# Top-k attention and a gated feed-forward: the comparison with the 32nd largest score moves from VectorE to GpSimd

## The chip, the core and the metric

The kernel runs on one core of a Trainium2 chip. A core has a matrix engine (TensorE, PE in the profile), a vector engine (VectorE, DVE), an engine for activation functions and copies (ScalarE, ACT), GpSimd (POOL) and a queue that issues transfers (SyncE, SP). Each engine works through its own instructions in program order, and they wait for one another through semaphores. The metric is the time of one execution on the device in microseconds (us), as the median of several runs; less is better. Beside the runs there is one profiled execution, from which all the lines of the profile come.

## What is computed

There are two parts. Attention over 8 batches and 8 heads, with 576 positions and a head size of 64, keeps for each query only the 32 largest scores; its output becomes the rows of a feed-forward layer of 4608 tokens, 512 wide, with 1536 hidden units.

```python
scores = scale * np.matmul(q, k.transpose(0, 1, 3, 2))          # scale = 1/8
kth = np.partition(scores, -32, axis=-1)[..., -32:-31]           # the 32nd largest
mask = scores >= kth
scores = np.where(mask, scores, -1e9)
attn = np.exp(scores - scores.max(-1, keepdims=True))
attn = attn / (attn.sum(-1, keepdims=True) + 1e-9)
x = np.matmul(attn, v)                                           # then (B,H,S,D) -> (B*S, H*D)
g = x @ w_gate
out = (g / (1 + np.exp(-g))) * (x @ w_val) @ w_out
```

All of it is float32.

## The kernel before

**Units.** Attention is cut into units of one batch, one tile of 128 queries and one pair of heads. 576 is four tiles of 128 and a rest of 64, so for each batch and pair there are four units of 128 queries with two heads each, and a fifth in which the 64 remaining queries of both heads share the 128 partitions, which then counts as one head. That makes 160 units, 128 with two heads and 32 with one. A head's scores are a row of 576 in each partition.

**A unit's way through the engines.** `scores` (L278) multiplies on TensorE and ScalarE copies the scores into the tile `sc`, which has two buffers. `select` (L316) works on VectorE alone: four rounds for each head, in which MAX8 (L329) finds the eight largest values and MATCH_REPLACE8 (L333) takes them out, so that the last value of the tile `m` is the 32nd largest. At the end of `select`, L339 writes a penalty into the tile `e`: the score is compared with the 32nd largest, and the result of the comparison, 1 or 0, is multiplied by FAR, -3e38. `penalize` (L343) works on GpSimd: it makes the bias for the exponential from the largest score (L349) and adds the scores to the penalty (L351), in one instruction for both heads, in place in `e`. `weigh` (L354) is the exponential on ScalarE with the sum of each row; `normalize` (L368) takes the reciprocal on VectorE (L372) and multiplies on ScalarE (L375). `turn` (L377) transposes the weights on TensorE (L387) and copies them back with ScalarE (L388), and `values` (L398) multiplies with v and writes the result to the feed-forward's input `xT`.

**The feed-forward.** `feed` (L457) works on blocks of 256 tokens, 18 in all. The first products (L471) go to gate and value; ScalarE evaluates them (L496 to L503) and GpSimd multiplies (L499, L504). The second product, with `w_out`, is done in full for the first block (L517). For all others it is done by a scheme with seven partial products instead of eight (L557), for which GpSimd forms differences and sums of the hidden values beforehand (L564, L572, L577, L605) and sums of the results afterwards (L543). `piece` hands out parts of this work, whose cost is counted in credits; `on_act` and `on_pool` are lists of ScalarE and GpSimd work that is put off until they are flushed.

**The weights.** Until about 190 us the 36 pieces of the weights are loaded and rounded to a shorter mantissa, in three steps on ScalarE (L114 to L117), VectorE (a shift, L121) and GpSimd (L122, L123). They are handed out between the rounds of `select`, five of them for every two units.

**The order.** The loop at L729 writes out by hand in which order each engine meets its instructions; the last lines of the kernel fix it. In step n, VectorE selects in unit n; GpSimd first does `penalize` for unit n-1, then the feed-forward work that is put off in `on_pool`; ScalarE copies for `turn(n-3)` and `values(n-4)`, then does the exponential of unit n-1, then the score copies of unit n+1, then what the feed-forward needs, and the normalization of unit n-2. TensorE does the transposes of unit n-3, the values of unit n-4, the scores of unit n+1, and then pieces of the feed-forward. The tile `e` has four buffers and `m` has two. No transfer is issued from GpSimd.

Of the kernel before, what the change touches and what calls it, by code (L numbers as in the profile page):

```python
# [9 lines left out]
ALU = mybir.AluOpType  # L10
FP32 = mybir.dt.float32
# [4 lines left out]
P = 128  # L16
TOP_K = 32
LOWEST = -3.4028234663852886e38
FAR = -3.0e38
# [6 lines left out]
def kernel(  # L26
# [37 lines left out]
    nc = tc.nc  # L64
    B, H, S, D = q.shape
# [16 lines left out]
    work = ctx.enter_context(tc.tile_pool(name="work", bufs=2))  # L82
# [189 lines left out]
    state = {}  # L272

    def n_heads(qt):

        return 1 if qt == J else 2
# [39 lines left out]
    def select(n):  # L316

        nh = n_heads(units[n][1])
        sc = state[n]["sc"]
        m = small.tile([P, 2, TOP_K], FP32, tag="m", name="m", bufs=2)  # L320
        heads = [slice(t * S, (t + 1) * S) for t in range(nh)]
        rest = work.tile([P, 2 * S], FP32, tag="rest", name="rest", bufs=1)
        e = work.tile([P, 2 * S], FP32, tag="e", name="e", bufs=4)
        state[n] |= dict(m=m, e=e, heads=heads)
        cur = sc
        rounds = TOP_K // 8
        for r in range(rounds):
            for t, hs in enumerate(heads):
                nc.vector.max(m[:, t, 8 * r : 8 * r + 8], cur[:, hs])  # L329
                yield  # L330
            if r < rounds - 1:
                for t, hs in enumerate(heads):
                    nc.vector.match_replace(  # L333
                        rest[:, hs], m[:, t, 8 * r : 8 * r + 8], cur[:, hs], LOWEST
                    )
                    yield
                cur = rest
        for t, hs in enumerate(heads):
            nc.vector.tensor_scalar(  # L339
                e[:, hs], sc[:, hs], m[:, t, TOP_K - 1 : TOP_K], FAR, ALU.is_lt, ALU.mult  # L340
            )

    def penalize(n):  # L343

        st = state[n]
        sc, m, e, heads = st.pop("sc"), st.pop("m"), st["e"], st["heads"]
        nh = len(heads)
        bias = small.tile([P, 2], FP32, tag="bias", name="bias")
        nc.gpsimd.tensor_scalar_mul(bias[:, 0:nh], m[:, 0:nh, 0], -scale)  # L349
        every = slice(0, nh * S)  # L350
        nc.gpsimd.tensor_tensor(e[:, every], e[:, every], sc[:, every], ALU.add)  # L351
        st["bias"] = bias
# [376 lines left out]
    for n in range(NU + VALUES):  # L729
        nh = n_heads(units[n][1]) if n < NU else 1  # L730
        topk = select(n) if n < NU else no
        over[n - 1] = normalize(n - 1) if 0 <= n - 1 < NU else no
        nxt = scores(n + 1) if n + 1 < NU else no
# [17 lines left out]
        if 0 <= n - 1 < NU:  # L751
            penalize(n - 1)
# [84 lines left out]
```

## Time and profile before

| | |
|---|---|
| median of 3 runs | 1821.28 us (1821.05 to 1821.64) |
| span of the profiled execution | 1817.8 us |
| mean granted TensorE clock | 0.967 of full speed |
| ScalarE busy | 1218.7 us, 67% of the span |
| VectorE: MAX8, MATCH_REPLACE8, the comparison | 817.7, 634.6 and 177.2 us busy |
| GpSimd: score addition L351, products L499 and L504 | 383.1 and 277.8 us busy |
| transfers | 59.65 MB, mean 33 GB/s |

The span runs from the first to the last instruction of the profiled execution; the runs' times also hold what lies before and after it. In the page, a group of instructions is given by its line in the kernel, the engine, the operation and the tiles it writes and reads; then come the number of instructions, the busy time, the mean duration in ns, and the engine's idle time just before them with what ended most of it. In a timeline the columns are start, time until the end (both in us), engine, line, operation, tiles, and in brackets the idle time before with its releaser. Consecutive instructions of a kind are merged there into one line with their number. The slices cut the span into forty equal parts; a digit is the busy share in tenths, and 9 means 90% or more.

### The profile page before, as it was taken

The page shows a single profiled execution, that of the slowest core. Times are in us where ns is not written, and L with a number is a line of the kernel's source. Part 1 is how long each engine was busy: PE and PEld are TensorE (multiplying, and loading weights), DVE is VectorE, ACT ScalarE, POOL GpSimd, SP SyncE. Part 2 cuts the span into 40 slices and gives each one's busy share as a digit, 9 for nine tenths or more (in the row PEclk, how much of TensorE's full clock was granted, in tenths as well). Part 3 has the DMA queues.
Part 4 walks back from the last instruction along what each step waited for, and adds up shares of the span by engine and source line. Part 5 has one row for each costly group of instructions (what it writes and reads, how often), then busy time and mean ns, then how long its engine had stood idle before and what let it go on. Part 6 is the DMA issues. An engine that isn't in the chain of part 4 may idle for free.

```text
span 1817.8 us, 30526 instructions
## 1 busy us (share of the span) xinstructions
PE 1708.7 (94%) x10756; PEld 1409.2 (78%) x10756; DVE 1610.7 (89%) x3372; ACT 1218.7 (67%) x2977; POOL 1036.4 (57%) x930
## 2 busy tenths in 40 slices
PE   4458999899999899999999999999999999999999
PEld 2346778687788788887888878887888878888887
DVE  7999999999999799997999989998999989998400
ACT  6778666676667676666767676767676766675532
POOL 5788756455565645554455636564556554646354
PEclk6669999899999999999999999999999999999999
DMA  7432030002100030000300021000300011000000
GB/s 191 125 108 90 14 85 7 12 1 50 45 1 13 2 82 12 13 1 22 73 12 2 13 56 39 1 12 3 74 19 13 1 36 33 1 13 12 1 12 12
DMA packets 109305, 59.65 MB, mean 33 GB/s; under 512 B 88544, under 2 KB 96992, under 8 KB 109152
## 3 DMA queue, kind: packets, MB, share of 16 engines
q1 hardware_dynamic: 108016, 57.37, 12.1%
q8 instruction: 85, 1.39, 0.3%
q14 instruction: 68, 0.56, 0.1%
q10 hardware_dynamic: 1136, 0.33, 0.1%
HBM read 48.23 MB, written 9.44 MB: 32 GB/s over the span
## 4 chain that ended last, share of the span: by engine, by line
PE 86%; DVE 8%; ACT 2%; POOL 2%; issue 2%; DMA 0%; SPq 0%; ACTq 0%; POOLq 0%
PE f L471 41%; PE x_ps L557 9%; PE av L416 8%; PE etps L387 7%; PE s L308 7%; PE y_ps L557 7%; DVE m L329 3%; DVE rest L333 3%; PE s L294 2%; PE av L407 1%; PE o_ps L517 1%; PE kqps L263 1%; DVE size L121 1%; DVE e L339 0%; POOL p L543 0%
## 5 line engine op out<-in xcount | busy, mean ns | idle before, releaser
L329 DVE MAX8 m<-rest 128x8 f32<-128x576 f32 x864 | 612.7, 744 | 2.2
L351 POOL TENSOR_TENSOR e<-e,sc 128x1152 f32<-128x1152 f32 (+1 forms) x160 | 383.1, 2394 | 83.7 <-DVE e L339 76.3
L333 DVE MATCH_REPLACE8 rest<-m,rest 128x576 f32<-128x576 f32 x576 | 423.1, 740 | 0.0
L471 PE MATMUL f<-xT,wg 128*128 128x256 f32 x1728 | 401.6, 382 | 0.0
L471 PE MATMUL f<-xT,wv 128*128 128x256 f32 x1728 | 399.1, 382 | 0.0
L471 PEld LDWEIGHTS f<-xT,wg 128*128 128x128 f32 x1728 | 323.1, 190 | 62.6 <-issue 21.3
L471 PEld LDWEIGHTS f<-xT,wv 128*128 128x128 f32 x1728 | 324.5, 190 | 58.7 <-issue 16.6
L499 POOL TENSOR_TENSOR h<-h,half_g 128x512 f32<-128x512 f32 x108 | 138.2, 1280 | 292.7 <-ACT h L498 292.2
L329 DVE MAX8 m<-sc 128x8 f32<-128x576 f32 x288 | 205.0, 747 | 104.0 <-ACT sc L299 57.8
L388 ACT COPY et<-etps 128x512 f32<-128x512 f32 (+1 forms) x448 | 184.1, 483 | 131.0 <-PE etps L387 130.2
L360 ACT ACTIVATE e<-e,bias 128x576 f32<-128x576 f32 x288 | 222.1, 777 | 57.5 <-POOL e L351 57.2
L387 PE MATMUL etps<-ident,e 128*128 128x128 f32 (+1 forms) x1312 | 184.5, 286 | 79.3 <-POOL size L122 18.2
L504 POOL TENSOR_TENSOR h<-h,val 128x512 f32<-128x512 f32 x108 | 139.6, 1293 | 186.3 <-ACT val L503 186.1
L387 PEld LDWEIGHTS etps<-ident,e 128*128 128x128 f32 (+1 forms) x1312 | 159.6, 147 | 106.0 <-POOL size L122 20.7
L375 ACT ACTIVATE e<-e,tot 128x576 f32<-128x576 f32 x288 | 212.0, 790 | 0.9 <-DVE tot L372 0.9
L333 DVE MATCH_REPLACE8 rest<-m,sc 128x576 f32<-128x576 f32 x288 | 211.5, 740 | 0.0
L308 PE MATMUL s<-kqT 64*128 64x288 f32 x1024 | 178.8, 449 | 14.1 <-ACT kqT L268 8.3
L339 DVE TENSOR_SCALAR e<-sc,m 128x576 f32<-128x576 f32 x288 | 177.2, 651 | 3.4
L416 PE MATMUL av<-et,v 128*64 128x128 f32 (+1 forms) x2560 | 170.3, 278 | 0.0
L313 ACT COPY sc<-s 128x288 f32<-128x288 f32 x512 | 164.0, 402 | 2.9 <-PE s L308 2.9
L496 ACT ACTIVATE h<-f 128x512 f32<-128x512 f32 x108 | 65.2, 604 | 133.3 <-PE f L471 133.3
L416 PEld LDWEIGHTS av<-et,v 128*64 128x64 f32 x2560 | 134.1, 143 | 22.8 <-issue 6.8
(73 smaller groups left out, 2029.1 us busy)
## 6 DMA issues: line engine op xcount, KB each, us to landing
v<-in_v_dram SPq DMA_DIRECT2D x32, 256.0 KB, 2.9
kq_in<-in_k_dram SPq DMA_DIRECT2D x63, 128.0 KB, 2.8
kq_in<-in_q_dram SPq DMA_DIRECT2D x63, 128.0 KB, 3.0
w<-in_moe_w_gate_dram SPq DMA_DIRECT2D x12, 512.0 KB, 3.7
w<-in_moe_w_val_dram SPq DMA_DIRECT2D x12, 512.0 KB, 3.8
w<-in_moe_w_out_dram SPq DMA_DIRECT2D x12, 512.0 KB, 3.5
out_dram<-o SPq DMA_DIRECT2D x38, 128.0 KB, 2.4
out_dram<-o SPq DMA_DIRECT2D x16, 256.0 KB, 2.4
```

Of the source, the lines that this page charges most:

```text
L308: nc.tensor.matmul(ps[:, 0:half], slab[d, q0 : q0 + P], slab[d, k0 : k0 + half])
L329: nc.vector.max(m[:, t, 8 * r : 8 * r + 8], cur[:, hs])
L333: nc.vector.match_replace(rest[:, hs], m[:, t, 8 * r : 8 * r + 8], cur[:, hs], LOWEST)
L339: nc.vector.tensor_scalar(e[:, hs], sc[:, hs], m[:, t, TOP_K - 1 : TOP_K], FAR, ALU.is_lt, ALU.mult)
L351: nc.gpsimd.tensor_tensor(e[:, every], e[:, every], sc[:, every], ALU.add)
L360: nc.scalar.activation(e[:, hs], e[:, hs], AF.Exp, bias=bias[:, t : t + 1], scale=scale, accum_out=tot[:, t : t + 1],)
L375: nc.scalar.mul(e[:, hs], e[:, hs], tot[:, t : t + 1])
L387: nc.tensor.transpose(ps[0:kl, c * P : (c + 1) * P], e[:, k0 : k0 + kl], ident[:])
L388: nc.scalar.copy(et[0:kl, c0 : c0 + cn, :], ps[0:kl, 0 : cn * P].rearrange("p (c j) -> p c j", c=cn),)
L416: nc.tensor.matmul(av[hh * R : (hh + 1) * R, 0:ql], v_last[:, hh, :] if c == J else vt[:, hh, c, :], moving, start=last and c == 0, stop=c ...
L471: nc.tensor.matmul(ps[:, i, :], w[:, kc, m * P : (m + 1) * P], x[:, kc, :], start=(kc == 0), stop=(kc == KC - 1),)
L557: nc.tensor.matmul(ps, lhsT, T[i][m], start=m == 0, stop=m == MQ - 1)
```

## The change

The comparison is no longer the last step of `select` on VectorE but is done on GpSimd in `penalize`, between the bias and the addition. The operation, its operands and its shape, one instruction for each head, stay the same. The tile `e` is accordingly allocated in `penalize`, one step later.

```diff
@@ select
-        e = work.tile([P, 2 * S], FP32, tag="e", name="e", bufs=4)
-        state[n] |= dict(m=m, e=e, heads=heads)
+        state[n] |= dict(m=m, heads=heads)
...
-        for t, hs in enumerate(heads):
-            nc.vector.tensor_scalar(
-                e[:, hs], sc[:, hs], m[:, t, TOP_K - 1 : TOP_K], FAR, ALU.is_lt, ALU.mult
-            )
@@ penalize
-        sc, m, e, heads = st.pop("sc"), st.pop("m"), st["e"], st["heads"]
+        sc, m, heads = st.pop("sc"), st.pop("m"), st["heads"]
+        e = work.tile([P, 2 * S], FP32, tag="e", name="e", bufs=4)
+        st["e"] = e
         nh = len(heads)
         bias = small.tile([P, 2], FP32, tag="bias", name="bias")
         nc.gpsimd.tensor_scalar_mul(bias[:, 0:nh], m[:, 0:nh, 0], -scale)
+        for t, hs in enumerate(heads):
+            nc.gpsimd.tensor_scalar(
+                e[:, hs], sc[:, hs], m[:, t, TOP_K - 1 : TOP_K], FAR, ALU.is_lt, ALU.mult
+            )
         every = slice(0, nh * S)
         nc.gpsimd.tensor_tensor(e[:, every], e[:, every], sc[:, every], ALU.add)
```

## The prediction

> **What bounds the kernel now.** I read the page first (busy shares, the forty slices, the costliest groups), then the windows by stage, the chain of waits, the durations of the removed line, and the timeline engine by engine at the places where TensorE stands still.
>
> ```profile
> PE 1708.7 (94%) x10756; PEld 1409.2 (78%) x10756; DVE 1610.7 (89%) x3372; ACT 1218.7 (67%) x2977; POOL 1036.4 (57%) x930
> ...
> PE   4458999899999899999999999999999999999999
> ...
> DVE  7999999999999799997999989998999989998400
> ...
> L351 POOL TENSOR_TENSOR e<-e,sc 128x1152 f32<-128x1152 f32 (+1 forms) x160 | 383.1, 2394 | 83.7 <-DVE e L339 76.3
> ...
> L339 DVE TENSOR_SCALAR e<-sc,m 128x576 f32<-128x576 f32 x288 | 177.2, 651 | 3.4
> ```
>
> TensorE (PE) and VectorE (DVE) are both nearly full, but not in the same slices. In the first four, PE is at 4 to 8 tenths and DVE is full; after that PE is full to the end and DVE has holes. Windows (busy us and instructions of PE, its weight loads, DVE, ACT, POOL; then clock, DMA) put numbers on it:
>
> ```profile
> 100.00:140.00 40.00, 20.41 (x111) 15.62 (x111) 40.00 (x82) 33.20 (x77) 30.11 (x22) 0.66 0.36 105
> ...
> 230.00:1700.00 1470.00, 1445.20 (x9315) 1198.24 (x9312) 1378.39 (x2904) 1003.64 (x2500) 815.08 (x740) 0.99 0.09 23
> ```
>
> So there are two stages. The **ramp** (10.85 to 165.8 us) has little for PE yet; the chain of waits there runs along DVE's L329, L333, L339 and L121. In the **long stage** PE is busy 1445 of 1470 us and its chain runs along L471 and L557: DVE time saved there buys nothing, and a microsecond by which PE is held up is lost for good. Outside these the three places at 340 to 360 us matter, below.
>
> **What is removed.** L339, two instructions for a unit of two heads. Its durations (ns, least, median, most) and its stretches in two ramp steps:
>
> ```profile
> L339 DVE TENSOR_SCALAR e<-sc,m x288: 490/510/2035, 21.2 to 1722.0; 128x576 f32<-128x576 f32 x144
> ...
> 96.86 1.41 DVE L329 MAX8 m<-sc 128x8 f32<-128x576 f32 x2
> ...
> 108.53 1.81 DVE L339 TENSOR_SCALAR e<-sc,m 128x576 f32<-128x576 f32 x2
> 110.26 1.40 DVE L329 MAX8 m<-sc 128x8 f32<-128x576 f32 x2
> ...
> 120.65 1.15 DVE L339 TENSOR_SCALAR e<-sc,m 128x576 f32<-128x576 f32 x2
> 121.72 1.41 DVE L329 MAX8 m<-sc 128x8 f32<-128x576 f32 x2
> ```
>
> Two steps take 121.72 - 96.86 = 24.86 us, 12.43 each; the ramp is (165.8 - 10.85) / 12.43 = 12.5 steps. L339 holds DVE from 108.53 to 110.26 and from 120.65 to 121.72, together 2.80 us, so DVE alone would need 22.06 us for two steps without it, 1.40 less per step. In the long stage a clean pair is 0.92 us (941.77), and nothing is gained there.
>
> **What is added: the price c of one compare on GpSimd (POOL).** The trace has no 128x576 tensor_scalar there. From below: the one-input ident<-ident of 128x128 takes 292 ns and the bias of 128x2 a median 217, so (292 - 217) / 126 = 0.60 ns per element and c = 217 + 574 x 0.60 = 0.56 us. From above: the add at L351 in its 128x576 form takes 1.41 us, but it reads two tensors. A compare reads one and does two operations; the low row is a single record of a quarter of the size. I take the middle, **c = 0.98 us**, 1.96 for a unit of two heads, and keep 0.56 and 1.41.
>
> A rule speaks here. The Trainium skill (GPSIMD Engine Reference, section 4.1, Engine selection) says that GpSimd takes about twice VectorE's time for two inputs but is roughly at line rate for one; with its 1.2 GHz that gives an estimate of 576 / 1.2 = 0.48 us plus 0.22 as for the bias, 0.70, and by that the sum below would come out near -2 us. The same section advises against elementwise work on GpSimd, which is against this change altogether.
>
> **Ramp, term by term.** POOL in the same two steps (96.15 to 121.01): five weight pieces (L122 and L123, start to start 2.76, 2.69, 2.62, 2.76, 2.62) = 13.45, two adds at 2.65, two biases. The biases take 0.42 plus a gap of 0.5 while L339 runs; without it, 0.22. That is 13.45 + 5.30 + 0.44 = 19.2 us, and POOL's present idle time (1.8 and 2.5 us, waiting for pieces that DVE releases in mid step) is what the compares fill first. With 4c = 3.9: 23.1 us against 24.86, so POOL takes over as the bound from DVE and the step is 0.87 us shorter. One thing opposes: the shifts of L121 on DVE take 0.4 us but up to 1.42 when POOL is busy. With POOL never idle, all five could wait half of an L122 (0.65 us): DVE then needs 22.06 - 2.64 (what they take now) + 5 x 0.98 = 24.3, and only 0.27 a step is won. Ramp: 12.5 x (0.27 to 0.87) = -3.4 to -10.9, taken as **-7**. At c = 0.56 DVE binds at best: -17 to -3.4, taken -10. At 1.41 POOL needs 24.8: nothing.
>
> **Feed-forward out of work (338 to 360 us).** Here POOL waits 5.7 and 7.7 us for L339 and PE idles 8.2 us in three pieces. DVE works through three steps without a hole; 0.92 us less each: **-3** (nearer -1 at c = 1.41, since the compare is in the same line of waits).
>
> **Long stage.** POOL is only 57% busy, but it works in program order, and in the second products of each feed-forward block (L557) PE and POOL feed each other. There the score addition stands between POOL's differences, and L339 has long been done, so its removal gives nothing back and the whole 2c is added. One block (POOL, then PE):
>
> ```profile
> 520.68 2.11 POOL L564 TENSOR_TENSOR xT<-h 128x256 f32<-128x256 f32 x3
> 522.75 0.22 POOL L349 TENSOR_SCALAR bias<-m 128x2 f32<-128x2 f32 x1
> 522.92 2.64 POOL L351 TENSOR_TENSOR e<-e,sc 128x1152 f32<-128x1152 f32 x1
> 525.52 1.27 POOL L504 TENSOR_TENSOR h<-h,val 128x512 f32<-128x512 f32 x1
> 526.76 2.62 POOL L572 TENSOR_TENSOR h<-h 128x256 f32<-128x256 f32 x3
> ...
> 529.68 2.75 PE L557 MATMUL x_ps<-wo,h 128*128 128x256 f32 x12
> ```
>
> POOL has no gap. The third L572 ends at 529.38; the matmuls that need it, the fifth of twelve pieces in PE's group, start at 529.68 + 4 x 0.216 = 530.5: slack 1.15 us. Read the same way, with L564, L572 or L577 as the last to come, ten blocks (at 308, 520, 612, 716, 801, 995, 1093, 1372, 1560 and 1650 us) have 0.5 to 1.5 us, mean 1.15. Each loses 2c - 1.15 = 0.81 us: **+8**. (At c = 0.56 about +1, at 1.41 10 x 1.67 = +17.) The blocks at 424, 905, 1181, 1280 and 1458 have no addition in that line, or over 2 us; they cost nothing.
>
> Then the places with no slack, where PE waits for the weights' normalization, queued on ScalarE behind the exponential, which waits for POOL:
>
> ```profile
> 629.19 0.21 POOL L349 TENSOR_SCALAR bias<-m 128x2 f32<-128x2 f32 x1
> 629.36 2.61 POOL L351 TENSOR_TENSOR e<-e,sc 128x1152 f32<-128x1152 f32 x1
> ...
> 632.01 0.78 ACT L360 ACTIVATE e<-e,bias 128x576 f32<-128x576 f32 x1 [4.67 <-POOL e L351]
> ...
> 635.55 2.00 PE L387 MATMUL etps<-ident,e 128*128 128x128 f32 x9 [4.62 <-ACT e L375]
> ```
>
> Such are 458, 635, 1120 and 1398 us (two heads, 2c) and 1492 and 1752 us (one head, c): 10c = **+10** (5.6 and 14.1 at the ends). What else stands behind the exponential on ScalarE: the score copies of the next unit, for which DVE waits. DVE has 1.4 us a step in hand after the change, so their delay costs nothing; were PE not the bound, it would be up to 1.96 - 0.92 us a step. No DMA is issued on POOL; SP's stores wait for POOL's last additions, and two of them end the kernel, after the last compare by 70 us.
>
> **Sum.** -7 - 3 + 8 + 10 = +8 us on a span of 1817.8: 1826. The median of the runs, 1821.3, lies 3.5 above that span, so **1829.3 us**.
>
> **Rivals.** (1) The compare is cheap and the ramp wins: -17 (or -10) - 3 + 6.4 = -14 (or -7): **1807 to 1815**. It speaks for it that POOL idles 43% of the span and that the ramp is plainly DVE's. The mechanism is one number, c: with ramp and feed-forward gap at -11, the long stage must stay under 11, which it does up to about c = 0.73. (2) The compare costs what a two-input add costs, or more: 0 - 1 + 17 + 14 = +30: **1851**; from c = 1.42 on, 19.2 + 4c exceeds 24.86 and POOL makes the ramp longer too (at c = 2, 12.5 x 1.2 = 15 more, and some 49 in the long stage, 1885). For it: every long POOL row of this trace is at 2.1 ns per element. Against: those read two tensors. (3) All of it is hidden, gain and loss cancel: **1821**.
>
> **Numbers.** Forecast (c from 0.8 to 1.2, slower, own range 1824 to 1840) 0.40; rival 1 0.27; rival 2 0.20; rival 3 0.13. The range reaches down to rival 1 with half of its ramp gain lost and up to somewhat past rival 2: 1809 to 1856. A measurement of this kernel tells 0.2% (3.6 us) from no change; faster 0.27, same 0.13, slower 0.60.
>
> **What would show it.** A row for the compare on POOL with its mean: 0.8 to 1.2 us by forecast, under 0.73 for rival 1, 1.4 or more for rival 2. DVE's busy time falls by about 177 us and its idle time, waiting for ScalarE's score copies, grows. The ramp's step comes to 11.5 to 12.2 us, with POOL full there and L121's mean up. In the long stage, PE waits for POOL's L572, L577 or L564 where none are listed now, and longer for ACT e L375. I am wrong if PE's idle time after 230 us does not grow, or if the ramp does not shorten.

## The result and the profile after

| | before | after |
|---|---|---|
| median | 1821.16 us (4 runs, 1819.4 to 1821.64) | 2181.26 us (4 runs, 2181.11 to 2181.99) |
| span of the profiled execution | 1817.8 us | 2179.4 us |

The ratio is 1.1977 (95% interval 1.196 to 1.1994): the change makes the kernel slower by 360 us, a fifth. The forecast was 1829 us, with a range from 1809 to 1856. The sign was right, the size was far off, and the measured time lies outside the range.

From the page of the changed kernel (busy times, slices, the chain that ended last, and three groups; the lines of the kernel have moved by one, so L348 is the comparison, L352 the addition, L361 the exponential, L328 MAX8):

```profile
PE 1820.5 (84%) x10756; PEld 1468.0 (67%) x10756; DVE 1459.9 (67%) x3084; ACT 1211.3 (56%) x2977; POOL 1664.5 (76%) x1218
...
PE   3348897697989798888988887988888988898999
...
DVE  7887587777777587676867675767766767776410
...
POOL 6999878777787777777778767788777786878654
...
PE 40%; POOL 35%; ACT 9%; issue 8%; DVE 6%; DMA 1%; SPq 0%; POOLq 0%; DVEq 0%; ACTq 0%
...
L348 POOL TENSOR_SCALAR e<-sc,m 128x576 f32<-128x576 f32 x288 | 636.7, 2221 | 37.0 <-DVE m L328 12.9
...
L328 DVE MAX8 m<-sc 128x8 f32<-128x576 f32 x288 | 205.9, 752 | 602.8 <-ACT sc L313 460.8
L361 ACT ACTIVATE e<-e,bias 128x576 f32<-128x576 f32 x288 | 221.2, 769 | 629.4 <-POOL e L352 629.4
```

The last two groups in the page of the kernel before:

```profile
L329 DVE MAX8 m<-sc 128x8 f32<-128x576 f32 x288 | 205.0, 747 | 104.0 <-ACT sc L299 57.8
...
L360 ACT ACTIVATE e<-e,bias 128x576 f32<-128x576 f32 x288 | 222.1, 777 | 57.5 <-POOL e L351 57.2
```

Three things are to be seen. One comparison on GpSimd takes 2.22 us, where VectorE took 0.65 in the mean. No engine is full any more after the ramp: from 205 to 2050 us PE is busy 87% of the time, POOL 77%, DVE 70%. And the idle time has a pattern: ScalarE waits 629 us for GpSimd's addition (57 before), VectorE waits 603 us for ScalarE's score copies (104 before). That is not the picture of one engine with too much work, but of engines that wait for one another in turn. Only the ramp looks different (window from 10 to 205 us: busy time and instructions of PE, weight loads, DVE, ACT, POOL, then clock, DMA):

```profile
10.00:205.00 195.00, 94.73 (x512) 72.66 (x509) 161.65 (x325) 138.76 (x309) 182.69 (x120) 0.68 0.40 111
```

GpSimd is busy 182.7 of 195 us there: in the ramp it is the bound by the amount of its work.

One step of the long stage, from the timelines of GpSimd, ScalarE, TensorE and VectorE:

```profile
1461.97 0.23 POOL L346 TENSOR_SCALAR bias<-m 128x2 f32<-128x2 f32 x1
1462.29 4.40 POOL L348 TENSOR_SCALAR e<-sc,m 128x576 f32<-128x576 f32 x2
1466.78 2.62 POOL L352 TENSOR_TENSOR e<-e,sc 128x1152 f32<-128x1152 f32 x1
1469.36 1.27 POOL L500 TENSOR_TENSOR h<-h,half_g 128x512 f32<-128x512 f32 x1
1473.21 1.28 POOL L505 TENSOR_TENSOR h<-h,val 128x512 f32<-128x512 f32 x1 [2.57 <-ACT val L504]
1474.57 0.23 POOL L346 TENSOR_SCALAR bias<-m 128x2 f32<-128x2 f32 x1
...
1469.44 0.78 ACT L361 ACTIVATE e<-e,bias 128x576 f32<-128x576 f32 x1 [6.12 <-POOL e L352]
1470.21 0.76 ACT L361 ACTIVATE e<-e,bias 128x576 f32<-128x576 f32 x1
1471.10 0.30 ACT L366 ACTIVATE tot<-tot,eps 128x2 f32<-128x2 f32 x1
1471.30 1.28 ACT L313 COPY sc<-s 128x288 f32<-128x288 f32 x4
1472.45 0.62 ACT L504 COPY val<-f 128x512 f32<-128x512 f32 x1
...
1473.84 1.38 PE L388 MATMUL etps<-ident,e 128*128 128x128 f32 x9 [2.78 <-issue]
...
1466.63 1.41 DVE L328 MAX8 m<-rest 128x8 f32<-128x576 f32 x2
```

Read it in a circle. GpSimd compares and adds from 1461.97 to 1469.40. ScalarE had waited 6.12 us for that; it does the exponential, the sum's step and the score copies of the next unit, and only then, in its program order, the copy L504 of the feed-forward's value, done at 1473.07. GpSimd had waited 2.57 us for this copy, multiplies, and only then, in its own program order, meets the comparisons of the next unit at 1474.57. The next unit's largest scores had been ready for 6.5 us: VectorE's last MAX8 ended at 1468.04. So a step lasts 7.4 (bias, comparisons, addition) + 3.6 (ScalarE) + 1.3 (product) + 0.3 (starts) = 12.6 us, whatever the engines could do otherwise. Where the gate's three ScalarE instructions stand in place of the value's copy it is 13.6. I call this **the ring**. The kernel before has the same ring without the comparisons: 7.9 to 8.8 us, hidden below TensorE's work for a step, which is 10.4 to 10.7 us in about half of the two-head steps without second products. There it is TensorE for which ScalarE waits before it copies the value:

```profile
1240.21 0.58 ACT L503 COPY val<-f 128x512 f32<-128x512 f32 x1 [1.30 <-PE f L471]
```

The table takes the time from one score addition to the next, by the timelines' starts, for the 159 steps that both kernels have in the same order. A step belongs to the second products if GpSimd does any of their differences and sums in it; three last steps, which nothing changes, are left out. A step counts as one of two heads if both its additions are for two heads. Steps without second products are called plain below.

| steps | number | before, mean us | after, mean us | difference in all |
|---|---|---|---|---|
| ramp (weights are rounded) | 14 | 12.84 | 15.20 | +33 |
| two heads, no second product | 63 | 10.99 | 13.07 | +131 |
| two heads, with second products | 43 | 11.73 | 15.49 | +162 |
| one head, no second product | 23 | 8.42 | 8.72 | +7 |
| one head, with second products | 13 | 7.71 | 9.34 | +21 |

With 4 us by which the first addition is later and 4 more behind the last, that is the whole loss. Of the 63 plain steps of two heads, 24 last 12.6 us and 30 last 13.5 or 13.6 after the change: the two lengths of the ring.

The steps with second products have no such length. There TensorE now waits for GpSimd's differences and sums (total us, number, longest), for which it waited 1.0 us in all before:

```profile
PE x_ps L558 <- POOL h L573: 27.2, 8, 5.6
PE x_ps L558 <- POOL xT L565: 17.9, 7, 3.8
PE x_ps L558 <- POOL h L606: 12.8, 5, 3.9
```

TensorE is also busy 112 us longer for the same 10756 instructions (a transpose takes 308 ns in the mean instead of 286), and its granted clock in five windows from 205 to 2050 us is 0.93 to 0.95, where it was 0.98 to 1.00 between 205 and 1690 us before. The ring of the plain steps does not hold TensorE; in the steps with second products this may be part of the loss, and no run separates it.

### The profile page after: what moved, and what is told of

The parts are those of the page before. It is cut to its first block, busy times and chain, and to the rows that moved or that the text cites. A ratio compares the mean times of both kernels' runs of the same rounds, so it can differ in the third digit from the quotient of the medians.

```text
span 2179.4 us, 30284 instructions
## 1 busy us (share of the span) xinstructions
PE 1820.5 (84%) x10756; PEld 1468.0 (67%) x10756; DVE 1459.9 (67%) x3084; ACT 1211.3 (56%) x2977; POOL 1664.5 (76%) x1218
## 3 DMA queue, kind: packets, MB, share of 16 engines
q1 hardware_dynamic: 108016, 57.37, 10.2%
## 4 chain that ended last, share of the span: by engine, by line
PE 40%; POOL 35%; ACT 9%; issue 8%; DVE 6%; DMA 1%; SPq 0%; POOLq 0%; DVEq 0%; ACTq 0%
PE f L472 23%; POOL e L348 16%; POOL e L352 9%; PE etps L388 5%; PE av L417 4%; ACT e L361 3%; PE s L308 3%; DVE m L328 3%; DVE rest L332 3%; PE x_ps L558 2%; ACT sc L313 2%; POOL size L122 2%; POOL h L505 1%; POOL h L500 1%; PE y_ps L558 1%
## 5 line engine op out<-in xcount | busy, mean ns | idle before, releaser
L348 POOL TENSOR_SCALAR e<-sc,m 128x576 f32<-128x576 f32 x288 | 636.7, 2221 | 37.0 <-DVE m L328 12.9
L328 DVE MAX8 m<-rest 128x8 f32<-128x576 f32 x864 | 614.1, 747 | 2.2
L328 DVE MAX8 m<-sc 128x8 f32<-128x576 f32 x288 | 205.9, 752 | 602.8 <-ACT sc L313 460.8
L361 ACT ACTIVATE e<-e,bias 128x576 f32<-128x576 f32 x288 | 221.2, 769 | 629.4 <-POOL e L352 629.4
L388 PE MATMUL etps<-ident,e 128*128 128x128 f32 (+1 forms) x1312 | 213.0, 308 | 247.1 <-issue 117.8
L352 POOL TENSOR_TENSOR e<-e,sc 128x1152 f32<-128x1152 f32 (+1 forms) x160 | 381.0, 2381 | 13.4
L388 PEld LDWEIGHTS etps<-ident,e 128*128 128x128 f32 (+1 forms) x1312 | 167.9, 156 | 299.9 <-issue 137.8
L308 PE MATMUL s<-kqT 64*128 64x288 f32 x1024 | 189.1, 463 | 13.3 <-ACT kqT L268 8.6
L417 PE MATMUL av<-et,v 128*64 128x128 f32 (+1 forms) x2560 | 189.8, 299 | 0.0
L417 PEld LDWEIGHTS av<-et,v 128*64 128x64 f32 x2560 | 151.0, 156 | 25.5 <-issue 12.2
L558 PE MATMUL x_ps<-wo,h 128*128 128x256 f32 x408 | 112.3, 428 | 40.0 <-POOL h L573 27.2
```

Source lines behind the costliest of these rows:

```text
L308: nc.tensor.matmul(ps[:, 0:half], slab[d, q0 : q0 + P], slab[d, k0 : k0 + half])
L348: nc.gpsimd.tensor_scalar(e[:, hs], sc[:, hs], m[:, t, TOP_K - 1 : TOP_K], FAR, ALU.is_lt, ALU.mult)
L361: nc.scalar.activation(e[:, hs], e[:, hs], AF.Exp, bias=bias[:, t : t + 1], scale=scale, accum_out=tot[:, t : t + 1],)
L388: nc.tensor.transpose(ps[0:kl, c * P : (c + 1) * P], e[:, k0 : k0 + kl], ident[:])
L417: nc.tensor.matmul(av[hh * R : (hh + 1) * R, 0:ql], v_last[:, hh, :] if c == J else vt[:, hh, c, :], moving, start=last and c == 0, stop=c ...
```

## The experiments

**Position alone.** `cmp_front` and `cmp_behind` have the same instructions and differ in one thing: in `cmp_behind` the tile `spare` and the loop of comparisons stand behind the addition. Both, like `no_compare` and the `dose` runs below, have three buffers for `e` instead of four; what that alone does was not tried. Each was run once; the kernels that were run several times vary by 0.3% at most. The edit of `cmp_front` against the changed kernel:

```diff
-        e = work.tile([P, 2 * S], FP32, tag="e", name="e", bufs=4)
+        e = work.tile([P, 2 * S], FP32, tag="e", name="e", bufs=3)
...
+        spare = work.tile([P, 2 * S], FP32, tag="spare", name="spare", bufs=1)
         for t, hs in enumerate(heads):
             nc.gpsimd.tensor_scalar(
-                e[:, hs], sc[:, hs], m[:, t, TOP_K - 1 : TOP_K], FAR, ALU.is_lt, ALU.mult
+                spare[:, hs], sc[:, hs], m[:, t, TOP_K - 1 : TOP_K], FAR, ALU.is_lt, ALU.mult
             )
         every = slice(0, nh * S)
-        nc.gpsimd.tensor_tensor(e[:, every], e[:, every], sc[:, every], ALU.add)
+        nc.gpsimd.tensor_tensor(e[:, every], sc[:, every], sc[:, every], ALU.add)
```

> No comparison on VectorE; the two comparisons run on GpSimd in front of the addition as in the changed kernel, but into a spare tile that nobody reads, and the addition adds the scores to themselves: the mask is left out. It is the base for the next kernel. Both theories: the time of the changed kernel, 2170 to 2195 us, since instructions, order and shapes are the same; a comparison takes 2.2 us.

Measured: 2098.4 us, 83 us less than the changed kernel and 72 below the range expected. The addition of a tensor to itself takes 2.11 us where that of two tensors takes 2.63. The ring's step accordingly came to 12.0 and 12.9 us instead of 12.6 and 13.6. So the expectation missed, and the miss itself fits the ring: the two-head steps are each 0.6 to 0.7 us shorter, 68 of the 83 us.

> The same instructions on GpSimd as in the run named cmp_front, but the two comparisons stand behind the addition instead of in front of it; the mask is left out here too. Theory of the ring: the changed kernel's step of 12.6 us is a ring in program order, GpSimd's comparisons and addition (7.4 us), ScalarE's exponential, score copies and value copy (3.6), GpSimd's product (1.3), and again. Behind the addition the 4.4 us of comparisons run beside ScalarE's 3.6, the ring falls to about 9 us, below TensorE's 10.5 to 11.4 us of work in a step, and the long stage is TensorE's again; what stays is the ramp (GpSimd 28 us for two steps) and delays in the second products: 1880 to 1930 us. Rival, the amount of work on GpSimd (and its sharing of the memory port) sets the time, wherever the work stands: 2170 to 2195 us as in cmp_front.

Measured: 1930.5 us, 168 us less than `cmp_front`, at the upper edge of what the ring theory gave and far from the rival's. The plain steps of two heads fell from 12.45 to 11.33 us, those with them from 14.83 to 13.45. GpSimd's busy time is the same in both (1586 and 1587 us). The amount of work on GpSimd is therefore not what makes these 168 us. From the timelines of GpSimd and ScalarE of `cmp_behind`:

```profile
1410.02 2.11 POOL L348 TENSOR_TENSOR e<-sc 128x1152 f32<-128x1152 f32 x1
1412.22 4.41 POOL L351 TENSOR_SCALAR spare<-sc,m 128x576 f32<-128x576 f32 x2
...
1412.16 0.78 ACT L362 ACTIVATE e<-e,bias 128x576 f32<-128x576 f32 x1 [0.62 <-POOL e L348]
...
1416.66 1.31 ACT L313 COPY sc<-s 128x288 f32<-128x288 f32 x4 [2.55 <-POOL spare L351]
```

The exponential now runs beside the comparisons. What I had not thought of is the last line: the comparisons still read `sc`, and the next score copies wait for that buffer. A smaller ring stays, 10.2 and 11.1 us in most of the plain steps, and these lose 22 us against the kernel before the change. More is lost in the two-head steps with second products, 74 us, and in the ramp, 25. Why those 74 us stay with the comparisons behind the addition, no run shows; the comparisons still stand ahead of GpSimd's differences and sums in program order.

**The gain alone.** `no_compare` is `cmp_front` without any comparison and without `spare`; the mask is left out here too.

> VectorE's comparison is taken away and none is added: the mask is left out, the addition adds the scores to themselves. This is the change with its gain alone. By the terms of the prediction the ramp gains up to 17 us and the place where the feed-forward runs out of work 3 us, the long stage nothing: 1800 to 1815 us. Rival: VectorE bounds more than the ramp (it is busy 89% of the span, and 0.92 to 1.4 us less in each of 144 steps is 130 to 200 us): under 1780 us.

Measured: 1801.6 us, ratio 0.9885 (0.9869 to 0.9902), 19.7 us faster, as the terms of the prediction had it. It is not the gain quite alone, since its addition of a tensor to itself is 0.5 us shorter. By the steps of the profiled executions, which differ by 16.7 us, 15 us of the gain lie in the ramp and ahead of its first addition, and 1.5 where the feed-forward runs out of work. VectorE's busy time falls by 161 us to 1449.9, and only 20 of them are worth anything: two steps of the ramp take 12.3 + 9.7 = 22.0 us, where the prediction had 22.06.

**Half the dose.** In `half_cmp` the first head is compared on GpSimd, the second on VectorE.

```diff
@@ select
         for t, hs in enumerate(heads):
+            if t == 0:
+                continue
...
@@ penalize
+        nc.gpsimd.tensor_scalar(
+            e[:, heads[0]], sc[:, heads[0]], m[:, 0, TOP_K - 1 : TOP_K], FAR, ALU.is_lt, ALU.mult
+        )
         every = slice(0, nh * S)
```

> The first head's comparison is on GpSimd, the second head's stays on VectorE; the result is the full one. Theory of the ring: 8 to 9 us of ring as before the change plus one comparison of 2.2 and its start is 10.3 to 11.3 us, about what TensorE has to do in a step, so most of the loss is gone: 1840 to 1880 us. Rival, each comparison on GpSimd costs its own time: half of the loss, 1990 to 2010 us.

Measured: 1930.7 us, ratio 1.0599 (1.0584 to 1.0615), between the two expectations. The ring came out as expected:

```profile
1400.70 0.23 POOL L351 TENSOR_SCALAR bias<-m 128x2 f32<-128x2 f32 x1
...
1410.73 1.28 POOL L504 TENSOR_TENSOR h<-h,half_g 128x512 f32<-128x512 f32 x1 [1.93 <-ACT h L503]
1412.10 0.23 POOL L351 TENSOR_SCALAR bias<-m 128x2 f32<-128x2 f32 x1
```

11.4 us with the gate's product, 10.4 with the value's; the 63 plain steps of two heads lose only 17 us. But the 43 with second products lose 64 us, 1.5 each in the mean, two thirds of the 2.2 us that are added, the 13 of one head 15, and the ramp 8. That is what my expectation lacked.

**What makes the comparison dear.** `forms` puts rows of four instructions on GpSimd in front of the kernel before.

> The kernel before the change, with rows of four instructions each on GpSimd put in front of everything, on one tile of 128x576: the comparison and multiplication as in the change (and at 128x288); the same against a constant in place of a column of m; the comparison alone, against a column and against a constant; subtraction and multiplication, subtraction and minimum, against a column; subtraction and multiplication with constants; one multiplication or one minimum; the addition of two tensors. Their results are read by nobody; the total time is of no interest. Theory: the comparison makes it dear, and the arithmetic forms take 0.7 to 1.1 us with two operations and no more with one, the comparisons 2.2 us. Rival one: two operations in one instruction make it dear, then all forms with two take about 2.2 us and those with one about half. Rival two: the column as an operand makes it dear, then the forms with constants take 0.7 to 1.1 us.

From the answer for the tile that they write (line, engine, operation, number, then the least, median and most duration in ns, first and last start, shape; `fm` is the column):

```profile
L110 POOL TENSOR_SCALAR fo<-fi,fm x4: 2208/2218/2236, 2.8 to 9.7; 128x576 f32<-128x576 f32 x4
L112 POOL TENSOR_SCALAR fo<-fi x4: 2134/2134/2137, 12.0 to 18.7; 128x576 f32<-128x576 f32 x4
L114 POOL TENSOR_SCALAR fo<-fi,fm x4: 1721/1721/2430, 20.9 to 27.1; 128x576 f32<-128x576 f32 x4
L116 POOL TENSOR_SCALAR fo<-fi x4: 1646/1646/1646, 28.9 to 34.1; 128x576 f32<-128x576 f32 x4
L118 POOL TENSOR_SCALAR fo<-fi,fm x4: 2209/2211/2219, 35.8 to 42.7; 128x576 f32<-128x576 f32 x4
...
L124 POOL TENSOR_SCALAR fo<-fi x4: 1647/1648/1656, 61.2 to 66.4; 128x576 f32<-128x576 f32 x4
...
L130 POOL TENSOR_TENSOR fo<-fi x4: 1144/1144/1145, 84.6 to 88.3; 128x576 f32<-128x576 f32 x4
L132 POOL TENSOR_SCALAR fo<-fi,fm x4: 1247/1248/1258, 89.5 to 93.5; 128x288 f32<-128x288 f32 x4
```

Shown are, in order: comparison and multiplication with a column; with a constant; comparison alone with a column; with a constant; subtraction and multiplication with a column; one multiplication by a constant; a tensor added to itself; the change's form on 288 columns. Comparing is not dear: subtraction costs the same (2.21), so the theory fell. The column costs 0.08 us, so rival two fell too. The second operation costs 0.5 us, so rival one is right in part. But all forms with a scalar operand are dear; the cheapest, one multiplication, takes 1.65 us, more than the 1.41 of an addition of two different tensors of this size. From 288 to 576 columns it is 3.4 ns a column and 0.28 us to start. Why GpSimd is slower with a scalar than with a second tensor these runs do not show.

**Out of the ring on ScalarE.** `exp_late` is the changed kernel with the exponential moved behind the evaluation of the feed-forward's products.

```diff
-        if 0 <= n - 1 < NU:
-            weigh(n - 1)
         run(nxt)
...
         pieces(2)
         flush(on_act)
+        if 0 <= n - 1 < NU:
+            weigh(n - 1)
```

> The changed kernel, with the exponential of unit n-1 moved on ScalarE behind the first evaluation of the feed-forward's products in step n; nothing on GpSimd changes and the result is the full one. Theory of the ring: the exponential (1.9 us with the sum's step) leaves the ring of comparisons, addition, score copies, value copy and product; the step of 12.6 to 13.6 us falls to 10.7 to 11.7, and 140 steps by 1.5 to 1.9 us are won: 1900 to 1980 us. Rival, GpSimd's work sets the time: 2175 to 2190 us, as the changed kernel.

Measured: 2057.2 us, ratio 1.1291 (1.1271 to 1.131), 124 us less than the changed kernel. Nothing was changed on GpSimd, so the rival falls again. The step is what the ring theory gave, start to start of the bias; on ScalarE the score copies and the value's copy now stand ahead of the exponential:

```profile
1407.23 0.23 POOL L346 TENSOR_SCALAR bias<-m 128x2 f32<-128x2 f32 x1
...
1418.09 0.23 POOL L346 TENSOR_SCALAR bias<-m 128x2 f32<-128x2 f32 x1
...
1414.70 1.31 ACT L313 COPY sc<-s 128x288 f32<-128x288 f32 x4 [3.02 <-POOL e L352]
1416.00 0.59 ACT L504 COPY val<-f 128x512 f32<-128x512 f32 x1
1416.48 0.78 ACT L361 ACTIVATE e<-e,bias 128x576 f32<-128x576 f32 x1
```

10.86 us; 11.7 with the gate's product. The expected time was too low, as the plain steps of two heads win 1.35 us in the mean (from 13.07 to 11.72), those with second products 0.9 (from 15.49 to 14.60), and those of one head and the ramp nothing.

**Gain and cost together.** `both_cmp` keeps VectorE's comparison and adds GpSimd's.

> The kernel before the change with its comparison on VectorE kept, and the two comparisons on GpSimd added in front of the addition, writing the same values again: the change with its cost alone. Theory of the ring: what VectorE is spared is worth nothing once GpSimd bounds the ramp and the ring the long stage, so the time is that of the changed kernel, 2175 to 2195 us. Rival, gain and cost add up: the 20 us that taking the comparison away brought are missing, 2198 to 2210 us.

Measured in one run: 2202.0 us, 20.8 more than the changed kernel, the rival's figure. I had thought that what VectorE is spared is worth nothing once others bind. The steps of the ramp lose another 6 us, those of one head 7 and the others 8; GpSimd waits 27 us in all for VectorE's comparison. That the sum agrees with the 20 us of `no_compare` need not mean the same places: there the gain lies mostly in the ramp.

**The forecast's price, made true.** `dose98` and `dose56` compare only so many columns that one comparison takes the 0.98 and 0.56 us of the prediction: 208 and 83. The edit of `dose98` against the changed kernel:

```diff
+    spare = consts.tile([P, 2 * S], FP32, name="spare")
+    nc.gpsimd.memset(spare[:], 0.0)
...
-        e = work.tile([P, 2 * S], FP32, tag="e", name="e", bufs=4)
+        e = work.tile([P, 2 * S], FP32, tag="e", name="e", bufs=3)
...
         for t, hs in enumerate(heads):
+            part = slice(t * S, t * S + 208)
             nc.gpsimd.tensor_scalar(
-                e[:, hs], sc[:, hs], m[:, t, TOP_K - 1 : TOP_K], FAR, ALU.is_lt, ALU.mult
+                spare[:, part], sc[:, part], m[:, t, TOP_K - 1 : TOP_K], FAR, ALU.is_lt, ALU.mult
             )
...
-        nc.gpsimd.tensor_tensor(e[:, every], e[:, every], sc[:, every], ALU.add)
+        nc.gpsimd.tensor_tensor(e[:, every], spare[:, every], sc[:, every], ALU.add)
```

> As the change, but each comparison on GpSimd covers only 208 of the 576 columns, which by the rows of the run forms (1.25 us for 288 columns, 2.22 for 576) is 0.98 us, the price that the prediction took; the result goes to a tile of zeros which is added to the scores, so that the mask is left out. VectorE's comparison is gone. If only the price was wrong, the prediction's sum comes true: 1824 to 1840 us. Rival, from the steps of the runs so far (a step with a second product loses what is added on GpSimd less about 0.75 us, in each of 43 steps of two heads, not in ten; the ring is 10.2 to 11.2 us): 43 x 1.4 = 60, the steps of one head 10, the ramp -9: 1865 to 1895 us.

The row of GpSimd's groups (busy us, mean ns, idle before):

```profile
L352 POOL TENSOR_SCALAR spare<-sc,m 128x208 f32<-128x208 f32 x288 | 281.6, 988 | 47.1 <-DVE m L331 17.5 <-ACT kqT L262 6.7 <-ACT sc L302 4.5
```

The price is 0.99 us as wanted, and the time 1887.6 us, ratio 1.0365 (1.0349 to 1.0381), 58 us above the forecast for this price. The 43 two-head steps with second products lose 52 us, the 13 of one head 10, the plain ones of two heads 11, while those of one head win 9; the ramp gains nothing (+3).

> The same with 83 columns, by the same rows 0.56 us each, the lowest price in the prediction; the mask is left out. By the prediction's terms 1807 to 1815 us, faster. By the steps of the runs so far: 43 x 0.55 = +24, the ramp -12, the ring 9.2 to 10.2 us and so hidden: 1822 to 1843 us.

Measured: 1839.9 us, ratio 1.0107 (1.0093 to 1.012), a comparison at 0.60 us. At the lowest price of the prediction, where it had 1807 to 1815 us, the change is still slower: the ramp gains 6 us and the plain steps of one head 8, the steps with second products lose 34.

**A mixture.** `ramp_mix` is the kernel before with six comparisons of the ramp on GpSimd, where it had idle time.

```diff
+EARLY = (2, 4, 6, 8, 10, 12)
...
+            if t == 0 and n in EARLY:
+                continue
...
+        if n in EARLY:
+            nc.gpsimd.tensor_scalar(
+                e[:, heads[0]], sc[:, heads[0]], m[:, 0, TOP_K - 1 : TOP_K], FAR, ALU.is_lt, ALU.mult
+            )
```

> The kernel before the change, with the first head's comparison of the units 2, 4, 6, 8, 10 and 12 on GpSimd and all others on VectorE; the result is the full one. In the ramp GpSimd has about 5 us to spare in two steps, most of it in the step with two weight pieces, which is where these six comparisons go. Theory of the ring (the ramp is VectorE's as long as GpSimd's sum for two steps, 19.2 + 2.4 us, is under VectorE's 24.1): 0.4 to 0.7 us less for two steps, 1816 to 1820 us. Rival, the comparison delays the exponential and with it the next scores: 1822 to 1830 us.

Measured: 1825.8 us, ratio 1.003 (1.0019 to 1.0041): a little slower. VectorE's timeline over two steps, and two instructions of GpSimd in the same time:

```profile
87.28 1.41 DVE L330 MAX8 m<-sc 128x8 f32<-128x576 f32 x2
...
97.85 0.53 DVE L342 TENSOR_SCALAR e<-sc,m 128x576 f32<-128x576 f32 x1
...
102.41 1.37 DVE L122 TENSOR_SCALAR size<-size 128x512 int32<-128x512 int32 x1
...
106.88 1.35 DVE L122 TENSOR_SCALAR size<-size 128x512 int32<-128x512 int32 x1
...
112.67 1.41 DVE L330 MAX8 m<-sc 128x8 f32<-128x576 f32 x2
...
100.86 2.64 POOL L358 TENSOR_TENSOR e<-e,sc 128x1152 f32<-128x1152 f32 x1
...
106.67 1.28 POOL L123 TENSOR_TENSOR size<-size,w 128x512 int32<-128x512 int32 x1
```

25.4 us instead of 24.9. The comparison is shorter, but two of the five shifts of the weights now take 1.35 us and the others 0.41, where before it was one in two steps. Both long shifts began while an instruction of GpSimd ran and ended 0.3 us after it (103.78 after 103.50, 108.23 after 107.95). Over the whole kernel 15 of the 36 shifts took more than 1 us, 7 before. What counts is where they fall: in the changed kernel, with GpSimd busier still, only 6 did. The Trainium skill (SBUF — State Buffer, section Who interferes with whom) says that VectorE's scalar forms can take a pair of memory ports that GpSimd uses, and that the later of the two then waits for the whole instruction; this agrees with it. The theory named the bound rightly and not what happens to it; the time is not its 1816 to 1820. It lies in the rival's range, but not for the rival's reason: VectorE works through the two steps with no wait for scores. So of the versions with the full result none is faster than the kernel before.

## Why the prediction was right and wrong

**What bounds the kernel before: right.** The two stages, VectorE in the ramp and TensorE after it, are confirmed by `no_compare`: 161 us less work for VectorE bring 20, most of them in the ramp.

**What the removal is worth: right in sum.** -17 in the ramp at best and -3 where the feed-forward runs out of work; 19.7 us measured, of which about 15 and 1.5 in these two places, with an addition that was shorter too.

**The price c: the first step that failed.** "From above: the add at L351 in its 128x576 form takes 1.41 us, but it reads two tensors." I took for granted that an instruction with one tensor and a scalar can't take longer than one with two tensors. The comparison takes 2.22 us, outside both ends, and the low end came from a single short record of another operation (292 ns for 128 columns), whose slope of 0.60 ns a column was wrong by more than five times. The estimate of 0.70 us worked out from the Trainium skill (GPSIMD Engine Reference, section 4.1, Engine selection) disagrees with the measured 2.22 too, and even with the 1.65 of a single operation; the measurement decides. That section's advice against elementwise work on GpSimd is borne out: 2.22 us here against 0.65 in the mean on VectorE.

**The ramp's formula: right, with the wrong c.** 19.2 + 4 x 2.22 = 28.1 us for two steps; measured 15.8 + 12.9 = 28.7. With c = 0.98 the gain was -7, and `dose98` had none. There the worst case for the shifts of L121 came true: 1.00 us in the mean instead of 0.62, and 13.60 + 10.91 = 24.5 us for two steps, where that case gave 24.3 and the kernel before takes 24.9. The last four steps of the ramp, in which GpSimd also multiplies for the feed-forward, lost 5 us, and for them the sum had no term.

**The long stage's slack: wrong at each price that was tried.** "Each loses 2c - 1.15 = 0.81 us: +8" was counted for ten blocks with one place each. A block of second products spreads over two to three steps, and each has a score addition between POOL's work and PE's. The runs show a loss in most of the 43 two-head steps (in 36 of them in `dose98` and `half_cmp`, in 41 in the changed kernel). In the mean of all 43 it is 1.2 us, 1.5 and 3.8, so all but 0.7 to 1.0 us of what is added. How this divides among PE's waits, the ring and PE's own longer work stays open. At the forecast's own c that is 62 us with the steps of one head, not 18. As for the six places with no slack, the trace lists a wait of PE for the normalization at 635, 1492 and 1752 us; at 458 it waits 1.55 us for the score copies, and at 1120 and 1398 PE itself has no gap.

**What was not there at all: the ring.** "What else stands behind the exponential on ScalarE: the score copies of the next unit, for which DVE waits. DVE has 1.4 us a step in hand after the change, so their delay costs nothing." Behind the score copies stands the value's copy, for which GpSimd waits before it reaches the next comparison. I had followed the wait to VectorE and stopped. By the prediction's own terms with c = 2.22 the sum would be 20 (ramp) + 33 + 22 = +75, some 1896 us. If 33 and 22 are put to the steps with second products, then of the other 285 us 131 lie in the plain steps of two heads, which is the ring, and 7 in those of one head; 128 lie in the steps with second products, and 17 in the ramp and ahead of it. At the forecast's own price the ring would have stayed nearly hidden: in `dose98` the plain steps of two heads lose 11 us. It is at the true price that it costs 131.

**The rivals.** Rival 2 had the direction (the comparison costs a two-input add or more), and its 1885 us at c = 2 shows again that the price alone doesn't explain the time. Rival 1 put the turning point at c = 0.73; by `dose56` it lies below 0.60. Of the signs named beforehand, DVE's busy time (-151 us; -177 were said), L121's mean (0.62 to 0.82 us), PE's waits for L572, L564 and L577 (27, 18 and 5 us) and GpSimd full in the ramp came; PE's idle time after 230 us grew from 26 to 248 us. The ramp did not shorten, which was one of the two signs of being wrong.

## What to carry to other kernels

When an engine that works in program order gets longer instructions ahead of something that others wait for, follow the wait until it comes back to the same engine: the length of that circle, not the engine's busy share, is what must stay below the step of the bound. Here 57% busy looked like room, and in the plain steps the circle of 7.9 to 8.8 us under a step of 10.4 to 10.7 us had room for about 2; in the steps with second products more than half of even 2 x 0.60 us was lost. And where an operation's price has no row of its own on the engine it moves to, neither a shorter row nor one with more inputs bounds it; take the far end wide.

## What the runs showed of the hardware

- On GpSimd an instruction with one tensor and a scalar took 1.65 to 1.72 us (one operation) or 2.13 to 2.22 us (two) on 128x576 float32; adding two tensors took 1.41, and a tensor to itself 1.14 (`forms` and the kernel before). Comparison, subtraction and minimum cost the same.
- Reading the same tensor twice instead of two tensors is 0.52 us less for an addition of 128x1152 on GpSimd: 2.11 us in `cmp_front` against 2.63 in the changed kernel and in `dose98`. Most of the 83 us between `cmp_front` and the changed kernel go with it.
